# Sliding-window attention and a squared-ReLU feed-forward layer on one core: a planned schedule with other DMA figures, stores issued on ScalarE, and accumulator rows zeroed by VectorE

## The chip, the cores and the metric

The kernel runs on one core of a Trainium2 chip. The time is that of the device for one execution, in microseconds (us). A core has five engines with an instruction queue each: TensorE (PE in the profile, its weight loads PEld), VectorE (DVE), ScalarE (ACT), GpSimd (POOL) and SyncE (SP). Each works through its queue in order and waits on semaphores.

## The reference

```python
# q, k, v: 8 batches x 8 heads x 576 positions x 64, float32
scores = q @ k^T / 8                     # per batch and head
attn = softmax(scores where |i - j| <= 32, else -1e9)
a = attn @ v                             # 8 x 8 x 576 x 64
x = a.transpose(0, 2, 1, 3).reshape(4608, 512)
out = relu(x @ w_in)**2 @ w_out          # w_in 512 x 2048, w_out 2048 x 512; out 4608 x 512 float32
```

## The kernel before

**Groups.** The 4608 rows of x are cut into 24 groups of 192 queries (G = 0 to 23), three to a batch (b, g = divmod(G, 3)). Each group treats all eight heads. A group has two halves w of 128 keys: half A (w = 0) and half B (w = 1). Because of the window of 32 to either side, the 128 keys of a half meet at most 128 queries other than zero.

**Attention of a group.** `load_qk` and `load_v` (L319, L331) load two pieces each of K, Q and V from GpSimd, which casts them to bf16. Q and K have to be transposed. For the first two batches (G below 6) TensorE does it (`turn_pe`, L361); after that SyncE issues transposing DMAs (`turn_dma`, L389, two of K and two of Q per group). `scores` (L400) runs eight matmuls per half into one PSUM tile; ScalarE takes the exponential (L426) and VectorE multiplies by the mask (L431). `pv` (L434) multiplies by V, with a 65th column of ones that gives the sum of each row. Rows 64 to 127 of the result of half A are final for the first 64 queries; rows 0 to 63 go on to half B. VectorE takes reciprocals (L464) and normalises (L467) into `xa` and `xb`. Between the halves, rows 64 to 127 of the PSUM tile `avp` must be made empty, since half B accumulates onto it: two small matmuls with zeros and start=True, one for each bank, ahead of half B's eight (L444). `xturn` (L472) transposes the result into columns of `xt`: by TensorE for G below 6 (`NXT`), by two transposing DMAs on SyncE from there on (L496, L498).

**Feed-forward.** `mm1` (L503) is the first projection: chunks of 192 tokens up to 768, one of 256, then 512; four matmuls of 128 x 128 weights per 128 of the 2048 features. ScalarE does the ReLU (L521) out of two PSUM buffers `ht`, VectorE the square (L524) into `gt`. `mm2` (L528) is the second projection for 128 tokens (block u, 36 in all) in four segments of four matmuls, into two PSUM buffers `outp`; after the last segment ScalarE copies the result into `oe` (L545), one of three buffers, and SyncE issues its store (L547).

**The order.** Nothing is ordered by hand. `rec` records each operation with what it reads and writes, a key and an assumed duration. The keys count in units of 64 tokens: first projection at its token's unit, second at 2u + LAG (LAG = 9), scores and P V of G at 3G - LEAD (LEAD = 12), the loads of a group AHEAD = 6 units before its scores. `schedule` then plans a run: an engine that is free takes the ready operation of lowest key. From this plan each engine's instruction list is written out, with semaphore waits for the dependences; on the chip an engine follows its list, whatever is ready. In the plan a DMA lands 1700 ns after its last packet is moved, a transposing DMA occupies SyncE for 900 ns:

```python
                    it[3].end = now + 1700
                    done(it[3], it[3].end)
```

A load of the third batch or later also waits, by `after=self.moe`, for the scores or first-projection operation recorded last before it. In the trace the loads of a group start some 1.1 us after the scores of half A two groups before it. Matmuls on zeros (L265) keep TensorE busy in gaps near the start.

Of the kernel before, what the change touches and what calls it, by code (L numbers as in the profile page):

```python
# [20 lines left out]
NTURN = 2  # L21
NXT = 6
LEAD = 12.0
LAG = 9.0
AHEAD = 6.0
WARM = 40000
KC = ((0, 224), (224, 192), (416, 160))


class Op:  # L30
    __slots__ = ("eng", "fn", "deps", "order", "inc", "val", "sem", "dma", "dur", "key", "i",
                 "succ", "left", "ready", "start", "end", "lat", "move", "name")


class Prog:
# [8 lines left out]
        self.writer = {}  # L44
        self.readers = {}

    def rec(self, eng, fn, reads=(), writes=(), dma=None, dur=100, key=0.0, move=0, name="", after=None):
        op = Op()
        op.eng, op.fn, op.dma, op.dur, op.key, op.move, op.name = eng, fn, dma, dur, key, move, name
        op.deps, op.order = set(), set()  # L50
        op.inc, op.val, op.sem = False, None, None
        op.lat = self.LAT[eng]
        for r in reads:
            w = self.writer.get(r)
            if w is not None:
                op.deps.add(w)
        for t in writes:
            w = self.writer.get(t)
            if w is not None:
                (op.order if w.eng == eng and w.dma is None and dma is None else op.deps).add(w)  # L60
            for r in self.readers.get(t, ()):
                (op.order if r.eng == eng and r.dma is None else op.deps).add(r)
        if after is not None:
            op.deps.add(after)
        op.deps.discard(op)
        op.order.discard(op)
        for r in reads:
            self.readers.setdefault(r, []).append(op)
        for t in writes:
            self.writer[t] = op  # L70
            self.readers[t] = []
        op.i = len(self.ops)
        self.ops.append(op)
        return op

    def schedule(self):
# [27 lines left out]
        def serve(until):  # L104
            nonlocal now, spent
            while now < until:
                nxt = min((r[0][0] for r in rings.values() if r), default=None)
                if nxt is None or nxt >= until:
                    now = max(now, min(until, nxt) if nxt is not None and nxt < 1e12 else until)
                    return False  # L110
                now = max(now, nxt)
                for q in list(order):
                    if rings[q] and rings[q][0][0] <= now:
                        break
                it = rings[q][0]
                spent += it[2]
                if spent >= (180 if q == "POOL" else 60):
                    order.remove(q)
                    order.append(q)
                    spent = 0  # L120
                now += it[2]
                it[1] -= 1
                if it[1] <= 0:
                    rings[q].pop(0)
                    it[3].end = now + 1700
                    done(it[3], it[3].end)
                    return True
            return False
# [87 lines left out]
def act(n):  # L216
    return 175 + 0.833 * n
# [6 lines left out]
class Gen:  # L224
# [5 lines left out]
    def alloc(self):  # L230
        nc = self.nc
        sb, ps = nc.alloc_sbuf_tensor, nc.alloc_psum_tensor
        self.SC = ps("sc", [128, 1024], F32)
        self.AVP = ps("avp", [128, 1024], F32)
        self.HT = [ps(f"ht{i}", [128, 512], F32) for i in range(2)]
        self.OUTP = [ps(f"outp{i}", [128, 512], F32) for i in range(2)]

        self.RAW = {t: [sb(f"{t}raw{i}", [128, 2, 512], BF16) for i in range(NRAW)] for t in "qk"}
        self.QT = [sb(f"qt{i}", [128, 4, S_], BF16) for i in range(2)]
        self.KT = [sb(f"kt{i}", [128, 4, KW], BF16) for i in range(2)]  # L240
        self.V = [sb(f"v{i}", [128, 2, H_, VS], BF16) for i in range(NV)]
        self.DIF = sb("dif", [128, 128], F32)
        self.MASK = [sb(f"mask{i}", [128, 128], BF16) for i in range(4)]
        self.ID = sb("ident", [128, 128], BF16)
        self.E = [sb(f"e{i}", [128, 1024], BF16) for i in range(2)]
        self.PT = [sb(f"pt{i}", [128, 8, 128], BF16) for i in range(3)]
        self.RS = [sb(f"rs{i}", [128, 8], F32) for i in range(4)]
        self.XA = [sb(f"xa{i}", [128, 512], BF16) for i in range(3)]
        self.XB = [sb(f"xb{i}", [128, 512], BF16) for i in range(3)]
        self.XT = sb("xt", [128, 4, RING], BF16)  # L250
        self.W1 = sb("w1", [128, 4, DFF], BF16)
        self.W2 = sb("w2", [128, 16, DM], BF16)
        self.GT = sb("gt", [128, 16, RING], BF16)
        self.RT = [sb(f"rt{i}", [128, 512], BF16) for i in range(4)]
        self.ZZ = sb("zz", [128, 512], BF16)
        self.OE = [sb(f"oe{i}", [128, 512], F32) for i in range(3)]

    def ms(self, eng, t, ap, v, key, dur=120):
        return self.p.rec(eng, lambda e: e.memset(ap, v), writes=t, key=key, dur=dur)  # L259
# [59 lines left out]
    def load_qk(self, t, b, g, key):  # L319
        t0, n = KC[g] if t == "k" else (192 * g, 192)  # L320
        h = n // 2
        G = 3 * b + g
        raw = self.RAW[t][G % NRAW]
        src = (self.q if t == "q" else self.k)[b]
        s = src[:, t0:t0 + n, :].rearrange("h (j p) d -> p j h d", j=2)
        for j in range(2):
            self.p.rec("POOL", lambda e, j=j: e.dma_start(raw[0:h, j, :].rearrange("p (h d) -> p h d", h=8), s[:, j]),  # L327
                       writes=[("raw", t, G % NRAW, j)], dma=(f"{t}{G % NRAW}{j}", G), key=key, dur=500 + 3 * h,
                       move=(h // 2, 14.5), name=f"{t}{b}{g}{j}", after=self.moe if b > 1 else None)

    def load_v(self, b, g, key):  # L331
        G = 3 * b + g
        vt = self.V[G % NV]
        for j in range(2):
            k0 = 192 * g - 32 + 128 * j
            lo, hi = max(k0, 0), min(k0 + 128, S_)
            n = hi - lo
            self.p.rec("POOL", lambda e, j=j, lo=lo, hi=hi, k0=k0: e.dma_start(  # L338
                vt[lo - k0:hi - k0, j, :, 0:64], self.v[b, :, lo:hi, :].rearrange("h p d -> p h d")),
                writes=[("v", G % NV, j)], dma=(f"v{G % NV}{j}", G), key=key, dur=500 + 3 * n, move=(n // 2, 14.5),  # L340
                name=f"v{b}{g}{j}", after=self.moe if b > 1 else None)

    def load_w1(self, d, key):
        src = self.w_in[:, 512 * d:512 * d + 512].rearrange("(f p) c -> p f c", p=128)
# [44 lines left out]
    def turn_dma(self, t, b, g, key):  # L389
# [3 lines left out]
        for x in range(2):  # L393
            self.p.rec("SP", lambda e, x=x: e.dma_start(dst[:, :, h * x:h * x + h], raw[0:h, x, :], transpose=True),  # L394
                       reads=[("raw", t, G % NRAW, x)], writes=[(t + "t", b % 2, g) if x else (t + "h", b % 2, g)],
                       dma=(f"t{t}{G % 6}", G), key=key, dur=900, move=(h // 4, 20), name=f"td{t}{b}{g}")

# [34 lines left out]
    def pv(self, G, w):  # L434
# [4 lines left out]


        def f(e):
            if w:
                for x in range(2):
                    e.matmul(avp[64:128, 512 * x + 508:512 * x + 512], self.ZZ[:, 0:64], self.ZZ[:, 0:4], start=True, stop=True,  # L444
                             skip_group_check=True)
# [7 lines left out]
        if G % 3 != 1:  # L453
            rd.append(("vpad", G % NV))
        wr = ["av_hi"] if w else ["av_hi", "av_lo"]
        self.p.rec("PE", f, reads=rd + (["av_lo"] if w else []), writes=wr + (["av_lo"] if w else []), key=key,
                   dur=260 + 100 * w, name=f"P{G}{'AB'[w]}")
        lo = 64 * (1 - w)
        rs = self.RS[n % 4]
        x = (self.XB if w else self.XA)[G % 3]  # L460
# [7 lines left out]
                                                    av[:, :, :, 0:64], rb, ALU.mult),  # L468
                   reads=rd + [("rs", n % 4)], writes=[("xb" if w else "xa", G % 3)], key=key - 0.05,
                   dur=dve(512, False), name=f"N{G}{'AB'[w]}")  # L470

    def xturn(self, G):  # L472
        xa, xb = self.XA[G % 3], self.XB[G % 3]
# [3 lines left out]
        if G < NXT:  # L477
# [7 lines left out]
            def f1(e):  # L485
                for j in range(4):
# [7 lines left out]
                       reads=["av_hi", "av_lo"], writes=wr, key=key, dur=act(768), name=f"XT{G}")  # L494
            return
        self.p.rec("SP", lambda e: e.dma_start(self.XT[:, :, r:r + 64], xa[64:128, :], transpose=True),  # L496
                   reads=[("xa", G % 3)], writes=wr[:1], dma=(f"xa{G % 3}", G), key=key - 0.3, dur=900, move=(16, 20), name=f"T{G}a")
        self.p.rec("SP", lambda e: e.dma_start(self.XT[:, :, r + 64:r + 192], xb[:], transpose=True),  # L498
                   reads=[("xb", G % 3)], writes=wr[1:], dma=(f"xb{G % 3}", G), key=key, dur=900, move=(32, 20), name=f"T{G}b")

# [25 lines left out]
    def mm2(self, u, seg, key):  # L528
# [12 lines left out]
        if u == 1 and seg == 0:  # L541
            self.p.idle_end = o
        if seg == 3:
            oe = self.OE[u % 3]
            self.p.rec("ACT", lambda e: e.activation(oe[:], op[:], ACTF.Copy), reads=[f"outp{u % 2}"],  # L545
                       writes=[("oe", u % 3)], key=key, dur=act(512), name=f"o{u}")
            self.p.rec("SP", lambda e: e.dma_start(self.out[128 * u:128 * u + 128, :], oe[:]),  # L547
                       reads=[("oe", u % 3)], writes=[("out", u)], dma=(f"o{u % 3}", u), key=key, dur=600, move=(8, 80), name=f"st{u}")

    def build(self):  # L550
        p = self.p
# [102 lines left out]
```

## Time and profile before

| what | value |
|---|---|
| median of three runs (lowest, highest) | 331.99 us (328.82, 335.5) |
| the profiled execution, its time | 333.94 us |
| its span, first to last instruction | 331.6 us |
| mean granted TensorE clock | 0.984 |
| busy: PE, DVE, ACT, POOL | 315.9, 142.5, 163.6, 120.8 us |
| first projection L515, PE busy | 148.6 us, 768 matmuls |
| second projection L535, PE busy | 145.3 us, 576 matmuls |
| scores L416, P V L448, clears L444, PE busy | 19.3, 20.7, 5.4 us |

Busy time of PE adds modelled ends of pipelined matmuls, which overlap: four matmuls of 512 columns that stand as 1.03 us start 0.216 us apart and give way to the next after 0.86 us. The stage from 151.5 to 247.5 us is steady: a group takes 12 us. Before 57 us no transposing DMA is issued; the last two for Q are issued from 247.45 us on; from 314.8 us TensorE does the second projection alone.

### The profile page before, as it was taken

The page shows a single profiled execution, that of the slowest core. Times are in us where ns is not written, and L with a number is a line of the kernel's source. Part 1 is how long each engine was busy: PE and PEld are TensorE (multiplying, and loading weights), DVE is VectorE, ACT ScalarE, POOL GpSimd, SP SyncE. Part 2 cuts the span into 40 slices and gives each one's busy share as a digit, 9 for nine tenths or more (in the row PEclk, how much of TensorE's full clock was granted, in tenths as well). Part 3 has the DMA queues.
Part 4 walks back from the last instruction along what each step waited for, and adds up shares of the span by engine and source line. Part 5 has one row for each costly group of instructions (what it writes and reads, how often), then busy time and mean ns, then how long its engine had stood idle before and what let it go on. Part 6 is the DMA issues. An engine that isn't in the chain of part 4 may idle for free.

```text
span 331.6 us, 6027 instructions
## 1 busy us (share of the span) xinstructions
PE 315.9 (95%) x2359; PEld 161.7 (49%) x2359; DVE 142.5 (43%) x332; ACT 163.6 (49%) x249; POOL 120.8 (36%) x157
## 2 busy tenths in 40 slices
PE   8999999949997999889999999999999999999996
PEld 3457786725643444344444444444444444444442
DVE  6356355704644547435354355355445432222200
ACT  1357575813724657355446545635544644434312
POOL 8999305632745519055145225325400000000000
PEclk9999999969999799999999999999999999999999
DMA  9999998999999999999999999799993120010012
GB/s 71 178 171 206 184 172 85 107 170 112 83 157 155 173 146 152 144 141 153 163 148 119 126 143 139 116 140 135 124 155 96 37 57 32 32 65 32 32 65 95
DMA packets 175451, 39.86 MB, mean 120 GB/s; under 512 B 166720, under 2 KB 170816, under 8 KB 175424
## 3 DMA queue, kind: packets, MB, share of 16 engines
q0 software_dynamic: 125312, 19.41, 89.5%
q1 hardware_dynamic: 50112, 20.07, 33.2%
q8 instruction: 19, 0.31, 0.4%
q14 instruction: 8, 0.07, 0.1%
HBM read 38.80 MB, written 9.44 MB: 145 GB/s over the span
## 4 chain that ended last, share of the span: by engine, by line
PE 85%; DMA 7%; SPq 3%; DVE 2%; ACT 1%; issue 1%; POOL 0%; POOLq 0%
PE ht L515 37%; PE outp L535 34%; DMA qt<-qraw 6%; PE sc L416 5%; PE avp L448 4%; PE outp L265 3%; SPq L394 2%; DMA kraw<-in_k_dram 1%; PE avp L444 1%; DVE xa L467 1%; DVE pt L431 1%; PE sc L374 1%; SPq L498 1%; PE avp L487 0%; PE avp L482 0%
## 5 line engine op out<-in xcount | busy, mean ns | idle before, releaser
L515 PE MATMUL ht<-xt,w 128*128 128x512 bf16 (+2 forms) x768 | 148.6, 329 | 0.5 <-ACT rt L521 0.2
L535 PE MATMUL outp<-w,gt 128*128 128x512 bf16 x576 | 145.3, 382 | 0.0
L521 ACT ACTIVATE rt<-ht 128x512 bf16<-128x512 f32 (+1 forms) x152 | 87.5, 576 | 93.1 <-PE ht L515 89.7
L524 DVE TENSOR_TENSOR gt<-rt 128x512 bf16<-128x512 bf16 (+1 forms) x152 | 61.7, 409 | 91.7 <-ACT rt L521 91.2
L515 PEld LDWEIGHTS ht<-xt,w 128*128 128x128 bf16 x768 | 67.3, 98 | 49.1 <-issue 1.1
L535 PEld LDWEIGHTS outp<-w,gt 128*128 128x128 bf16 x576 | 54.2, 98 | 62.2 <-issue 1.7
L327 POOL DMA_DIRECT2D kraw<-in_k_dram x48 | 37.9, 808 | 119.8 <-PE sc L416 69.4
L426 ACT ACTIVATE e<-sc 128x1024 bf16<-128x1024 f32 x48 | 49.1, 1022 | 26.3 <-PE sc L416 26.3
L431 DVE TENSOR_TENSOR pt<-e,mask 128x1024 bf16<-128x1024 bf16 x48 | 33.1, 689 | 44.8 <-ACT e L426 44.4
L338 POOL DMA_DIRECT2D v<-in_v_dram x48 | 41.6, 891 | 0.0
L327 POOL DMA_DIRECT2D qraw<-in_q_dram x48 | 37.7, 807 | 0.0
L545 ACT ACTIVATE oe<-outp 128x512 f32<-128x512 f32 x36 | 21.5, 597 | 30.3 <-PE outp L535 27.2
L416 PE MATMUL sc<-qt,kt 64*128 64x128 bf16 x384 | 19.3, 220 | 10.4 <-DMA qt<-qraw 10.2
L416 PEld LDWEIGHTS sc<-qt,kt 64*128 64x128 bf16 x384 | 11.0, 95 | 29.1 <-issue 14.7
L464 DVE RECIPROCAL rs<-avp 64x8 f32<-64x8 f32 (+1 forms) x48 | 10.0, 209 | 26.9 <-PE avp L448 26.5
L448 PE MATMUL avp<-v,pt 128*128 128x65 bf16 x384 | 20.7, 196 | 0.0
L448 PEld LDWEIGHTS avp<-v,pt 128*128 128x128 bf16 x384 | 16.6, 99 | 5.7 <-DVE pt L431 0.6
L265 PE MATMUL outp<-zz 128*128 128x512 bf16 x55 | 16.9, 430 | 1.2 <-DVE zz L259 1.2
L467 DVE TENSOR_TENSOR xb<-avp,rs 128x512 bf16<-128x512 f32 x24 | 16.6, 690 | 1.2
L467 DVE TENSOR_TENSOR xa<-avp,rs 64x512 bf16<-64x512 f32 x24 | 16.7, 695 | 0.9
L265 PEld LDWEIGHTS outp<-zz 128*128 128x128 bf16 x55 | 5.2, 106 | 6.5 <-issue 2.5
L492 ACT ACTIVATE xt<-avp 128x768 bf16<-128x768 bf16 x6 | 4.9, 810 | 6.0 <-PE avp L487 5.9
(35 smaller groups left out, 49.9 us busy)
## 6 DMA issues: line engine op xcount, KB each, us to landing
out_dram<-oe SPq DMA_DIRECT2D x36, 256.0 KB, 2.6
qraw<-in_q_dram POOLq DMA_DIRECT2D x48, 96.0 KB, 5.5
v<-in_v_dram POOLq DMA_DIRECT2D x32, 128.0 KB, 6.8
w<-in_moe_w_in_dram POOLq DMA_DIRECT2D x4, 512.0 KB, 8.9
w<-in_moe_w_out_dram POOLq DMA_DIRECT2D x4, 512.0 KB, 15.4
kraw<-in_k_dram POOLq DMA_DIRECT2D x16, 112.0 KB, 4.7
v<-in_v_dram POOLq DMA_DIRECT2D x16, 96.0 KB, 6.0
kraw<-in_k_dram POOLq DMA_DIRECT2D x16, 96.0 KB, 5.3
```

The lines of the kernel that those rows point to most:

```text
L265: self.p.idle = lambda e: e.matmul(self.OUTP[1][:], self.ZZ[:, 0:128], self.ZZ[:], start=True, stop=True)
L327: self.p.rec("POOL", lambda e, j=j: e.dma_start(raw[0:h, j, :].rearrange("p (h d) -> p h d", h=8), s[:, j]), writes=[("raw", t, G % NRAW, ...
L338: self.p.rec("POOL", lambda e, j=j, lo=lo, hi=hi, k0=k0: e.dma_start(vt[lo - k0:hi - k0, j, :, 0:64], self.v[b, :, lo:hi, :].rearrange("h ...
L416: mm = e.matmul(sc[:, 512 * par + 128 * j:512 * par + 128 * j + 128], kt[r:r + 64, j, k0:k0 + 128], q, start=True, stop=True)
L426: self.p.rec("ACT", lambda e: e.activation(e_[:], sc[:], ACTF.Exp, scale=0.125), reads=["sc0", "sc1"], writes=[("e", n % 2)], key=key, dur ...
L431: self.p.rec("DVE", lambda e: e.tensor_tensor(pt[:], ee, mb, ALU.mult), reads=[("e", n % 2), ("mask", mi)], writes=[("pt", n % 3)], key=ke ...
L448: mm = e.matmul(avp[:, 512 * x + 65 * y:512 * x + 65 * y + 65], pt[:, 4 * (h % 2) + h // 2, :], vt[:, w, h, 0:65], start=(w == 0 and y == ...
L467: self.p.rec("DVE", lambda e: e.tensor_tensor(x[lo:128, :].rearrange("p (x y c) -> p x y c", x=2, y=4), av[:, :, :, 0:64], rb, ALU.mult), ...
L515: mm = e.matmul(ht[:, n * x:n * x + n], self.W1[:, ft, 128 * d:128 * d + 128], self.XT[:, ft, r:r + n], start=(ft == 0), stop=(ft == 3))
L521: self.p.rec("ACT", lambda e: e.activation(rt[:, 0:c], ht[:, 0:c], ACTF.Relu), reads=[f"ht{k % 2}"], writes=[("rt", k % 4)], key=key, dur= ...
L524: self.p.rec("DVE", lambda e: e.tensor_tensor(gt[:, d0:d0 + len(ds), r:r + n], rr, rr, ALU.mult), reads=[("rt", k % 4)], writes=[("gt", s, ...
L535: mm = e.matmul(op[:], gt[:, d, r:r + 128], self.W2[:, d, :], start=(d == 0), stop=(d == 15))
```

## The change

Five things are changed together.

1. The plan's figures for transposing DMAs: an issue takes 1290 ns (`TISS`) where it was 900, and a landing 2000 ns more (`TSLACK`). For loads of the third batch on, a landing takes 1500 ns more (`LSLACK`). These change the planned order alone; no instruction waits longer by them.
2. The two clearing matmuls stay for G below 6 (`NCLR`). From G = 6 a VectorE memset of rows 64 to 127 and 2 x 260 columns of `avp` stands in for them. It reads `xa`, so it follows half A's normalisation, and half B's P V waits for it.
3. The store of the output is issued by ScalarE instead of SyncE.
4. `oe` has four buffers instead of three.
5. LAG is 6 instead of 9.

```diff
-LAG = 9.0
+LAG = 6.0
 AHEAD = 6.0
+TISS = 1290
+TSLACK = 2000
+LSLACK = 1500
+NCLR = 6
...
-                    it[3].end = now + 1700
+                    it[3].end = now + 1700 + it[3].slack
...
-        self.OE = [sb(f"oe{i}", [128, 512], F32) for i in range(3)]
+        self.OE = [sb(f"oe{i}", [128, 512], F32) for i in range(4)]
...
-                       move=(h // 2, 14.5), name=f"{t}{b}{g}{j}", after=self.moe if b > 1 else None)
+                       move=(h // 2, 14.5), name=f"{t}{b}{g}{j}", after=self.moe if b > 1 else None, slack=LSLACK if b > 1 else 0)
...
-                       dma=(f"t{t}{G % 6}", G), key=key, dur=900, move=(h // 4, 20), name=f"td{t}{b}{g}")
+                       dma=(f"t{t}{G % 6}", G), key=key, dur=TISS, move=(h // 4, 20), name=f"td{t}{b}{g}", slack=TSLACK)
...
-            if w:
+            if w and G < NCLR:
                 for x in range(2):
                     e.matmul(avp[64:128, 512 * x + 508:512 * x + 512], self.ZZ[:, 0:64], self.ZZ[:, 0:4], start=True, stop=True,
                              skip_group_check=True)
...
-                   dur=260 + 100 * w, name=f"P{G}{'AB'[w]}")
+                   dur=260 + 160 * (w and G < NCLR), name=f"P{G}{'AB'[w]}")
...
+        if not w and G >= NCLR:
+            z = avp[64:128, :].rearrange("p (x c) -> p x c", x=2)[:, :, 0:260]
+            self.p.rec("DVE", lambda e: e.memset(z, 0.0), reads=[("xa", G % 3)], writes=["av_hi"], key=key - 0.05, dur=650, name=f"Z{G}")
...
-            oe = self.OE[u % 3]
+            oe = self.OE[u % 4]
...
-            self.p.rec("SP", lambda e: e.dma_start(self.out[128 * u:128 * u + 128, :], oe[:]),
-                       reads=[("oe", u % 3)], writes=[("out", u)], dma=(f"o{u % 3}", u), key=key, dur=600, move=(8, 80), name=f"st{u}")
+            self.p.rec("ACT", lambda e: e.dma_start(self.out[128 * u:128 * u + 128, :], oe[:]),
+                       reads=[("oe", u % 4)], writes=[("out", u)], dma=(f"o{u % 4}", u), key=key, dur=600, move=(8, 80), name=f"st{u}")
```

The two transposing DMAs of `xturn` get `TISS` and `TSLACK` in the same way.

More of the change, by code (lines that the diff above doesn't have):

```diff
@@ L31 @@
     __slots__ = ("eng", "fn", "deps", "order", "inc", "val", "sem", "dma", "dur", "key", "i",
-                 "succ", "left", "ready", "start", "end", "lat", "move", "name")
+                 "succ", "left", "ready", "start", "end", "lat", "move", "name", "slack")
 class Prog:
@@ L45, in __init__, with rec @@
         self.readers = {}
-    def rec(self, eng, fn, reads=(), writes=(), dma=None, dur=100, key=0.0, move=0, name="", after=None):
+    def rec(self, eng, fn, reads=(), writes=(), dma=None, dur=100, key=0.0, move=0, name="", after=None, slack=0):
         op = Op()
@@ L51, in rec @@
         op.inc, op.val, op.sem = False, None, None
+        op.slack = slack
         op.lat = self.LAT[eng]
@@ L340, in load_v @@
                 writes=[("v", G % NV, j)], dma=(f"v{G % NV}{j}", G), key=key, dur=500 + 3 * n, move=(n // 2, 14.5),
-                name=f"v{b}{g}{j}", after=self.moe if b > 1 else None)
+                name=f"v{b}{g}{j}", after=self.moe if b > 1 else None, slack=LSLACK if b > 1 else 0)
     def load_w1(self, d, key):
@@ L496, in xturn @@
         self.p.rec("SP", lambda e: e.dma_start(self.XT[:, :, r:r + 64], xa[64:128, :], transpose=True),
-                   reads=[("xa", G % 3)], writes=wr[:1], dma=(f"xa{G % 3}", G), key=key - 0.3, dur=900, move=(16, 20), name=f"T{G}a")
+                   reads=[("xa", G % 3)], writes=wr[:1], dma=(f"xa{G % 3}", G), key=key - 0.3, dur=TISS, move=(16, 20), name=f"T{G}a",
+                   slack=TSLACK)
         self.p.rec("SP", lambda e: e.dma_start(self.XT[:, :, r + 64:r + 192], xb[:], transpose=True),
-                   reads=[("xb", G % 3)], writes=wr[1:], dma=(f"xb{G % 3}", G), key=key, dur=900, move=(32, 20), name=f"T{G}b")
+                   reads=[("xb", G % 3)], writes=wr[1:], dma=(f"xb{G % 3}", G), key=key, dur=TISS, move=(32, 20), name=f"T{G}b", slack=TSLACK)
     def mm1(self, t0, n, ds, key):
@@ L543, in mm2 @@
         if seg == 3:
-            oe = self.OE[u % 3]
+            oe = self.OE[u % 4]
             self.p.rec("ACT", lambda e: e.activation(oe[:], op[:], ACTF.Copy), reads=[f"outp{u % 2}"],
-                       writes=[("oe", u % 3)], key=key, dur=act(512), name=f"o{u}")
-            self.p.rec("SP", lambda e: e.dma_start(self.out[128 * u:128 * u + 128, :], oe[:]),
-                       reads=[("oe", u % 3)], writes=[("out", u)], dma=(f"o{u % 3}", u), key=key, dur=600, move=(8, 80), name=f"st{u}")
+                       writes=[("oe", u % 4)], key=key, dur=act(512), name=f"o{u}")
+            self.p.rec("ACT", lambda e: e.dma_start(self.out[128 * u:128 * u + 128, :], oe[:]),
+                       reads=[("oe", u % 4)], writes=[("out", u)], dma=(f"o{u % 4}", u), key=key, dur=600, move=(8, 80), name=f"st{u}")
     def build(self):
```

## The prediction

> **What bounds the kernel now.** I read the page's busy row and clock row first, then the waits of TensorE, then the span cut into stages around those waits, then the order of time on TensorE, SyncE and GpSimd inside them.
>
> ```profile
> PE 315.9 (95%) x2359; PEld 161.7 (49%) x2359; DVE 142.5 (43%) x332; ACT 163.6 (49%) x249; POOL 120.8 (36%) x157
> PEclk9999999969999799999999999999999999999999
> PE sc L416 <- DMA qt<-qraw: 10.2, 3, 5.4
> 65.47:71.02 5.55, 0.17 (x2) 0.04 (x2) 0.89 (x3) 0.60 (x1) 0.83 (x1) 0.77 2.05 168
> 71.02:75.34 4.32, 4.32 (x30) 2.43 (x30) 1.50 (x4) 1.51 (x2) 3.31 (x5) 0.50 1.13 152
> 105.90:108.13 2.23, 0.06 (x1) 0.00 (x1) 1.27 (x3) 0.00 (x0) 0.85 (x2) 1.00 1.46 240
> 109.48:112.89 3.41, 3.41 (x18) 1.59 (x18) 2.54 (x6) 2.34 (x4) 3.41 (x5) 0.50 1.99 147
> 139.40:142.08 2.68, 0.00 (x1) 0.00 (x1) 0.43 (x1) 0.60 (x1) 0.00 (x0) 1.00 1.74 149
> ```
>
> TensorE is the bound: it is busy 95% of the span, and from 142 us to the last matmul it never waits. (A stage row gives from:to, length, busy us with counts for PE, PEld, DVE, ACT and POOL, then clock, DMA share and GB/s.) So a change is worth what it takes from TensorE's own list or from its holes. The holes after the start are three, all in front of a score group (L416) that waits for a transposed Q: 10.2 us together. After two of them the granted clock is 0.50 for 4.32 and 3.41 us.
>
> ```profile
> 52.35 0.40 PE L416 MATMUL sc<-qt,kt 64*128 64x128 bf16 x8
> 53.48 1.64 POOL L327 DMA_DIRECT2D kraw<-in_k_dram  x2 [17.38 <-PE sc L416]
> 57.21 6.16 SPq L394 DMA_TRANSPOSE kt<-kraw  x2
> 63.41 2.56 SPq L394 DMA_TRANSPOSE qt<-qraw  x2
> 64.61 1.03 PE L535 MATMUL outp<-w,gt 128*128 128x512 bf16 x4
> 71.02 0.61 PE L416 MATMUL sc<-qt,kt 64*128 64x128 bf16 x8 [5.38 <-DMA qt<-qraw]
> 108.13 0.40 PE L416 MATMUL sc<-qt,kt 64*128 64x128 bf16 x8 [2.18 <-DMA qt<-qraw]
> 142.08 0.40 PE L416 MATMUL sc<-qt,kt 64*128 64x128 bf16 x8 [2.68 <-DMA qt<-qraw]
> ```
>
> This is one chain from end to end. Group 4's scores at 52.35 release the loads of group 6 on GpSimd (53.48); SyncE issues two transposes of K, held by the loads, then two of Q, done at 65.97; Q lands about 5 us later and group 6's scores start at 71.02, 18.67 us after group 4's. TensorE had come to that place at 65.64, 13.3 us after 52.35. The instruction order is fixed before the run by a planner, so TensorE can't take other work in the hole although projection work was ready: at 65.5 it had done about 3.9 of the four 192-token chunks of the first projection and 3 token blocks (48 matmuls) of the second, of six whose inputs the first four chunks give.
>
> **The three stalls.** The planner's figures in the code are 900 ns for a transposing issue and 1700 ns from last packet to landing. The trace has 1254 ns:
>
> ```profile
> L394 SPq DMA_TRANSPOSE qt<-qraw x36: 1180/1254/2522, 63.4 to 247.4; - x36
> L547 SPq DMA_DIRECT2D out_dram<-oe x36: 332/519/1682, 42.8 to 329.3; - x36
> ```
>
> The diff plans 1290 ns an issue (4 in the chain, so 4 x 0.39 = 1.56 us), 1.5 us more for a load and 2.0 us more for a transpose: the planned chain grows by 5.06 us. It doesn't make data earlier; it moves the score group later in TensorE's list, behind work that is ready. Against 5.38, 2.18 and 2.68 us of lateness it leaves 0.32, 0 and 0. Bounds on the spread: transposes land after 2.3 us at best, 5.0 at the median, 8.5 at worst. The new plan allows 0.6 + 0.5 + 1.7 + 2.0 = 4.8 us, so the worst is 3.7 late, of which the load and issue margins (1.5 + 1.56) catch 3.06: 0.64 us an event. I take two such events, 1.3 us; the ends are 0 and all three stalls as before. So 10.24 - 0.32 - 1.3 = 8.6 us gained.
>
> **The clock behind them.** TensorE worked 4.32 and 3.41 us at 0.50: 2.16 + 1.70 = 3.86 us lost. Without the holes I take all of it back; the least is nothing. The Trainium skill, page "TensorE: Matmul & The Clock Gate", section "Part 1: The HAM clock gate", speaks against a part of this: it lets the clock halve only after at least one whole idle window of about 3.4 us. By that rule the 2.18 us hole did not cause the second half-clock stretch and 1.70 us of this term would stay; here the trace has the stretch 1.35 us after that hole, and I go by the trace.
>
> **Clearing matmuls.** Groups 6 to 23 lose their pair (L444). In the steady stage:
>
> ```profile
> 190.86 0.42 PE L448 MATMUL avp<-v,pt 128*128 128x65 bf16 x8
> 191.12 1.02 PE L535 MATMUL outp<-w,gt 128*128 128x512 bf16 x4
> 192.84 1.03 PE L535 MATMUL outp<-w,gt 128*128 128x512 bf16 x4
> 193.80 0.22 PE L444 MATMUL avp<-zz 128*64 128x4 bf16 x2
> 193.95 0.43 PE L448 MATMUL avp<-v,pt 128*128 128x65 bf16 x8
> 194.22 1.02 PE L515 MATMUL ht<-xt,w 128*128 128x512 bf16 x4
> ```
>
> Four 512-column matmuls start 0.216 us apart, so the group of 192.84 gives way at 193.70; P V starts at 193.95. The half without a clear follows its neighbour with no gap (190.86 to 191.12 is its own 0.26 us, as 193.95 to 194.22 is). A pair costs 0.25 us of TensorE: 18 x 0.25 = 4.5 us.
>
> Its stand-in is a VectorE memset of 64 partitions x 520 f32 in PSUM. No row shows one. The nearest are
>
> ```profile
> L467 DVE TENSOR_TENSOR xa<-avp,rs 64x512 bf16<-64x512 f32 x24 | 16.7, 695 | 0.9
> L259 DVE MEMSET v<- 32x264 uint32 x4 | 1.1, 278 | 0.2
> ```
>
> so 0.28 to 0.70 us; scaled from the memset, 278 x 520/264 = 0.55, which I take. 18 x 0.55 = 9.9 us on VectorE, 45 us busy in the 96 us from 151.5 to 247.5. It lies between the normalisation of half A and P V of half B: a new wait of one memset and a hand-over. In the steady stage A ends at 191.28 and B starts 193.95; reciprocal, normalisation and memset (0.21 + 0.70 + 0.55, with three hand-overs of about 0.1 to 0.2) end near 193.1. What it can hold on VectorE is the next half's mask multiply and a squaring; TensorE has three projection groups of 0.86 us there. I price it at nothing; with no cover 18 x 0.7 = 12.6 us. A gain is excluded.
>
> **Stores on ScalarE.** SyncE loses 36 issues of about 0.52 us (18.7 us) and the waits in front of them; ScalarE gets them, each behind its own copy (L545). SyncE then carries six transposes a group, 6 x 1.25 = 7.5 of 12 us, and the Q of the next groups no longer stands behind a store. Queued behind the store on ScalarE are the next ReLU (L521) and exponential (L426), for which TensorE waits through two buffers: 1.73 us per turn when both projections alternate, of which ScalarE uses 0.60. ScalarE is busy 51.0 of 96 us; 0.52 more in 8 us fits. I take nothing; with no cover 18.7 us, and the gain's end is 0, since the only wait for a store (3.2 us, ScalarE at 108.7) lay beside a stall of TensorE. The fourth output buffer only loosens that wait.
>
> **LAG 9 to 6** ranks the second projection three units (192 tokens) earlier. It moves work within a list that is full: the tail after the last first-projection group shrinks from 63 matmuls to about 51 (an estimate: three units are 24 matmuls, half of them met by first-projection work that goes later), and the same matmuls run before. Nothing; if the last squaring were late, the other output buffer holds 0.86 us groups to run. The start, up to the first transposing issue at 57.21, keeps its loads: the slack applies from the third batch on.
>
> **Sum.** -8.6 - 3.9 - 4.5 = -17.0 us. The profiled execution took 333.94 (span 331.6 and 2.3 around it), 1.95 above the median of 331.99. From the median: 315.0; from the profiled one: 316.9. I give **315.0**.
>
> **Rivals.** *The cover runs out* (0.12). From 92.87 to 101.3 TensorE has only the second projection to do, waiting for group 7's columns; then 12 of that work's matmuls are left, 2.6 us. If TensorE comes there 5.38 + 2.16 us sooner and the columns don't, a hole of about 5 us opens: 320. Against it: group 7's Q landed near 75.6 while its scores ran at 84.11, late only because the list had slid by those 7.5 us.
>
> *Holes or blocked evictions stay* (0.12). The margins miss, or half the store issues (9.4 us) land on TensorE's path: 322 to 327.5; the upper end is the clears alone, the change not doing what it says. For it: loads and transposes together took 8 us to land around 130.
>
> *The attention chain becomes the bound* (0.10), on the slower side. Each group's loads wait for the scores two groups before. That chain is 18.7 us at group 6 and up to 21 later; TensorE needs 24 us for two groups now and 23.5 after. If the planned chain exceeds 23.5, TensorE starves once the ready work is used: at 26 us it loses 2.5 us in each of 8.5 links from group 6 to 23, 21 us, and -17 + 21 makes 336. Its point is 23.5 us, and 18.7 to 21 real plus margins that mostly equal the real lateness keep under it.
>
> The **forecast** has 0.66. Its own range is 310 (all 18.6 us and the lowest run's 328.8) to 319. To hold 8 in 10 I go up to 326, which takes in the cover case and most of the third. 2% is 6.6 us, about what a measurement of this kernel can tell from no change: faster 0.79, same 0.12, slower 0.09.
>
> **What would show it.** Right: no wait of L416 on Q over 1 us, clock 1.00 from 30 us on, 12 clearing matmuls, a group period near 11.75 us from 150 us on. Wrong: waits of P V on a memset, of L515 on ReLUs behind store issues, of L515 on transposed attention columns near 95 us, or a group period above 12 us.

## The result, and the profile after

The changed kernel takes 317.31 us (median of four runs, 316.5 to 318.14) where the kernel before takes 332.56 (328.82 to 335.5) on the same chip: a ratio of 0.958, interval 0.949 to 0.967. In a later comparison it was 317.08 against 329.77, ratio 0.964 (0.959 to 0.969). Here and below a ratio leaves out runs more than 1.5% above the fastest of their kernel, so it is not quite the quotient of the medians. The change takes 13 to 15 us; the forecast was 17, and 315.0 lies 2.3 us below the measured median. The profiled execution took 316.6 us with a span of 314.4.

The page's busy row and clock row, then the waits of TensorE on other engines, the longest first. Lines have moved by a few: scores are L421, clears L449, P V L453, the first projection L524, the second L544.

```profile
PE 303.9 (97%) x2284; PEld 158.8 (51%) x2322; DVE 149.7 (48%) x350; ACT 162.8 (52%) x249; POOL 120.6 (38%) x157
PEclk9999999999999999999999999999999999999999
PE outp L379 <- DMA kraw<-in_k_dram: 1.6, 2, 1.0
PE outp L270 <- DVE zz L264: 1.2, 1, 1.2
PE ht L524 <- issue: 0.8, 5, 0.2
```

No wait of scores on Q is left, and the clock is full in every slice. The waits on loads and on the zeros are those of the start. The rows that end with "issue" are gaps of 0.2 us: this trace has 2284 matmuls to 2322 weight loads, so 38 matmul records are missing, and such a gap is about one matmul long. In order of time, the place where the kernel before stood still for 5.38 us (groups 5 and 6):

```profile
67.96 0.43 PE L453 MATMUL avp<-v,pt 128*128 128x65 bf16 x8
68.22 1.89 PE L544 MATMUL outp<-w,gt 128*128 128x512 bf16 x8
...
71.36 1.03 PE L544 MATMUL outp<-w,gt 128*128 128x512 bf16 x4
72.32 0.40 PE L421 MATMUL sc<-qt,kt 64*128 64x128 bf16 x8
```

Group 6's scores start at 72.32, later than the 71.02 of before. The list now has P V of group 5 and second-projection work in front, and TensorE works through what was a hole.

The memset and its neighbours in the group and wait rows, and in order of time:

```profile
L478 DVE MEMSET avp<- 64x520 f32 x18 | 8.9, 492 | 2.3 <-DVE xa L472 0.9
PEld avp L453 <- DVE avp L478: 1.6, 6, 0.3
166.50 1.03 PE L524 MATMUL ht<-xt,w 128*128 128x512 bf16 x4
167.36 0.42 PE L453 MATMUL avp<-v,pt 128*128 128x65 bf16 x8
167.83 0.81 PE L544 MATMUL outp<-w,gt 128*128 128x512 bf16 x3
```

It takes 0.49 us (0.55 estimated). P V follows the projection with no gap in front (166.50 to 167.36 is four matmuls), as forecast. From 167.36 to 167.83 it seems to take 0.47 us instead of 0.26, but the group behind it has three matmuls where there are always four: the first one's record is missing. The second profile of the changed kernel has as many matmuls as weight loads (2322), and the same place in it reads

```profile
166.53 1.03 PE L524 MATMUL ht<-xt,w 128*128 128x512 bf16 x4
167.39 0.42 PE L453 MATMUL avp<-v,pt 128*128 128x65 bf16 x8
167.65 1.02 PE L544 MATMUL outp<-w,gt 128*128 128x512 bf16 x4
```

with 0.26 us, as before. In six of 18 groups the weight load of P V waited for the memset, 1.6 us together, but P V itself started late by 0.1 us at most.

Two-group spacing of scores shows who sets the pace. In the stage from 150 us on the kernel before kept 12.0 us a group, the pace of TensorE's list. Now group 14's scores are at 152.00 and group 16's at 172.89, 20.9 us for two: attention runs ahead of TensorE's need, and group 23's scores come at 247.64 instead of 259.49. Only the last two steps, from group 21 to 23, are even, 11.74 and 11.75 us.

### The profile page after: what moved, and what is told of

Read it like the earlier page. It is cut to its first block, busy times and chain, and to the rows that moved or that the text cites. A ratio compares the mean times of both kernels' runs of the same rounds, so it can differ in the third digit from the quotient of the medians.

```text
span 314.4 us, 5936 instructions
## 1 busy us (share of the span) xinstructions
PE 303.9 (97%) x2284; PEld 158.8 (51%) x2322; DVE 149.7 (48%) x350; ACT 162.8 (52%) x249; POOL 120.6 (38%) x157
## 4 chain that ended last, share of the span: by engine, by line
PE 86%; DMA 6%; POOL 3%; issue 1%; DVE 1%; ACT 1%; SPq 1%; ACTq 0%; POOLq 0%
PE ht L524 38%; PE outp L544 37%; PE sc L421 5%; PE avp L453 4%; DMA qt<-qraw 3%; DMA qraw<-in_q_dram 3%; POOL kraw L332 1%; SPq L399 1%; POOL qraw L332 1%; PE sc L379 1%; PE outp L270 1%; POOL v L343 1%; POOL w L350 0%; PE avp L495 0%; ACT rt L530 0%
## 5 line engine op out<-in xcount | busy, mean ns | idle before, releaser
L524 PE MATMUL ht<-xt,w 128*128 128x512 bf16 (+2 forms) x754 | 143.9, 325 | 1.3 <-issue 0.8
L544 PE MATMUL outp<-w,gt 128*128 128x512 bf16 x555 | 138.7, 379 | 1.3 <-issue 0.3
L533 DVE TENSOR_TENSOR gt<-rt 128x512 bf16<-128x512 bf16 (+1 forms) x152 | 60.8, 406 | 72.3 <-ACT rt L530 71.4
L524 PEld LDWEIGHTS ht<-xt,w 128*128 128x128 bf16 x768 | 67.3, 98 | 50.6 <-ACT rt L530 1.3
L544 PEld LDWEIGHTS outp<-w,gt 128*128 128x128 bf16 x576 | 53.4, 98 | 59.8 <-ACT oe L554 1.3
L453 PEld LDWEIGHTS avp<-v,pt 128*128 128x128 bf16 x384 | 17.5, 98 | 9.8 <-DVE avp L478 1.6
L453 PE MATMUL avp<-v,pt 128*128 128x65 bf16 x384 | 20.1, 194 | 0.3 <-DVE pt L436 0.3
L421 PE MATMUL sc<-qt,kt 64*128 64x128 bf16 x384 | 19.1, 219 | 0.4 <-ACT qt L388 0.3
L421 PEld LDWEIGHTS sc<-qt,kt 64*128 64x128 bf16 x384 | 10.9, 94 | 16.9 <-issue 8.2
L270 PE MATMUL outp<-zz 128*128 128x512 bf16 x51 | 15.1, 420 | 1.4 <-DVE zz L264 1.2
L478 DVE MEMSET avp<- 64x520 f32 x18 | 8.9, 492 | 2.3 <-DVE xa L472 0.9
```

Source lines behind the costliest of these rows:

```text
L421: mm = e.matmul(sc[:, 512 * par + 128 * j:512 * par + 128 * j + 128], kt[r:r + 64, j, k0:k0 + 128], q, start=True, stop=True)
L453: mm = e.matmul(avp[:, 512 * x + 65 * y:512 * x + 65 * y + 65], pt[:, 4 * (h % 2) + h // 2, :], vt[:, w, h, 0:65], start=(w == 0 and y == ...
L524: mm = e.matmul(ht[:, n * x:n * x + n], self.W1[:, ft, 128 * d:128 * d + 128], self.XT[:, ft, r:r + n], start=(ft == 0), stop=(ft == 3))
L533: self.p.rec("DVE", lambda e: e.tensor_tensor(gt[:, d0:d0 + len(ds), r:r + n], rr, rr, ALU.mult), reads=[("rt", k % 4)], writes=[("gt", s, ...
L544: mm = e.matmul(op[:], gt[:, d, r:r + 128], self.W2[:, d, :], start=(d == 0), stop=(d == 15))
```

## The experiments

The theory: TensorE's own work plus the holes in its list is the time; a hole is the lateness of transposed Q, K or attention columns against the planned order; the clock halves after some holes. Rivals: SyncE's queue is what is late; the memset gives back elsewhere what the clears cost; the long chain of attention is the bound.

### Single parts on the kernel before

The plan's figures alone:

```diff
+TISS = 1290      # dur of the four transposing DMA records, 900 before
+TSLACK = 2000    # their slack
+LSLACK = 1500    # slack of loads from the third batch on
-                    it[3].end = now + 1700
+                    it[3].end = now + 1700 + it[3].slack
```

> The kernel before with the plan's figures alone (1290 ns issues, 2000 and 1500 ns slack); clears, stores on SyncE, three output buffers and LAG 9 as before. The prediction's own sum: the three holes before scores and the half clock after them go, -12.5 us, near 320 us where the kernel before has 332; no wait of scores on Q over 1 us. Rival (SyncE's queue is what is late, because stores and their waits stand among the transposes): holes of several us stay, 326 to 332.

Measured 320.38 us against 329.83 for the kernel before, ratio 0.974 (0.970 to 0.979). Its profile has no wait of scores on a DMA at all. The holes and the clock behind them are cured by order alone, with every store still on SyncE; the rival falls as the main cause. The gain is 9.5 us and not 12.5. The three figures were changed together; which of them is needed is not shown.

The memset alone, for the clears of groups 6 to 23:

```diff
-            if w:
+            if w and G < NCLR:
...
+        if not w and G >= NCLR:
+            z = avp[64:128, :].rearrange("p (x c) -> p x c", x=2)[:, :, 0:260]
+            self.p.rec("DVE", lambda e: e.memset(z, 0.0), ...
...
-                   dur=260 + 100 * w, name=f"P{G}{'AB'[w]}")
+                   dur=260 + 160 * (w and G < NCLR), name=f"P{G}{'AB'[w]}")
```

The last lines are the planned duration of P V, which goes with the clears; it changes the order alone.

> The kernel before with VectorE's memset in place of the clears from group 6 on, and nothing else. The prediction's sum: 18 x 0.25 = 4.5 us less TensorE work, 327.5 where the kernel before has 332, if the three holes keep their 10.2 us. Rival (a change of the order moves the holes as well): a time outside 325 to 330, with holes whose sum differs from 10.2 us by as much.

Measured 330.12 us, ratio 1.000 (0.996 to 1.004): nothing. The sum's 327.5 fails; the time lies at the upper edge of the rival's range, and the holes did move. The work did leave TensorE: half A's scores of groups 16 and 17 in its steady stage are

```profile
173.21 0.40 PE L421 MATMUL sc<-qt,kt 64*128 64x128 bf16 x8
184.95 0.40 PE L421 MATMUL sc<-qt,kt 64*128 64x128 bf16 x8
```

11.74 us apart, the 0.26 us less that the clears' price says. It came back in holes and clock (waits, one row of the order of time, and one stage row, whose last three figures are clock, DMA share and GB/s):

```profile
PE sc L421 <- DMA qt<-qraw: 6.2, 3, 3.8
PE ht L524 <- DMA xt<-xb: 2.5, 2, 2.1
127.21 3.57 PE L524 MATMUL ht<-xt,w 128*128 128x512 bf16 x8 [2.10 <-DMA xt<-xb]
127.28:130.70 3.42, 3.42 (x11) 1.23 (x12) 0.00 (x0) 0.60 (x1) 3.38 (x5) 0.50 2.41 154
```

A new hole before the first projection waits for transposed attention columns, and half clock follows it; another 6.8 us of half clock stand at the hole of 3.8 us before scores. Over the runs of this comparison the mean granted clock is 0.983 with the memset (the 11 runs of its ratio) and 0.994 without (18 runs); one minus the clock, times the span, is 5.5 against 1.9 us. So up to 3.6 of the 4.5 us went to the clock (these figures count idle time at half clock too, which costs nothing). The rest may be longer holes, but a single profile can't show that.

Stores on ScalarE, four output buffers and LAG 6 together, plan's figures and clears as before:

```diff
-LAG = 9.0
+LAG = 6.0
-            oe = self.OE[u % 3]
+            oe = self.OE[u % 4]
-            self.p.rec("SP", lambda e: e.dma_start(self.out[...
+            self.p.rec("ACT", lambda e: e.dma_start(self.out[...
```

> The kernel before with stores on ScalarE, four output buffers and LAG 6; plan's figures and clears as before. The prediction's sum: nothing, 330 to 334, the holes before scores still there (10 us). Rival (SyncE freed of stores is the cure): holes under 5 us together, 320 to 326.

Measured 326.88 us, ratio 0.993 (0.989 to 0.997). Between the two expectations: 3 us gained, where I priced nothing. Its profile, of the fastest of twelve executions, has 2.0 us of waits of scores on Q, and 0.9 us on columns.

### The changed kernel less one part

The old plan's figures:

```diff
-TISS = 1290
-TSLACK = 2000
-LSLACK = 1500
+TISS = 900
+TSLACK = 0
+LSLACK = 0
```

> The changed kernel with the old plan's figures (900 ns, no slack). The prediction's sum: it loses the 12.5 us of holes and clock again, near 329.5. Rival (freed SyncE and moved stores have already made Q punctual): 317 to 322.

Measured 325.31 us against 329.83 for the kernel before (ratio 0.985, 0.979 to 0.991), some 8 us above the changed kernel of the next comparison (where the kernel before has 329.77). That lies between the two expectations: the old figures bring back 8 us, not 12.5. Its profile, of one of its two longest executions (327.21 us), has 4.7 us of waits of scores on Q. The other three were run beside the changed kernel on one chip, itself unedited:

> The changed kernel once more, as the measure for the three beside it: 314 to 318 where the kernel before has 330 to 332.

Measured 317.08 us.

```diff
-NCLR = 6
+NCLR = 24                                  # clears in all groups, no memset
...
-                   dur=260 + 160 * (w and G < NCLR), name=f"P{G}{'AB'[w]}")
+                   dur=260 + 100 * w, name=f"P{G}{'AB'[w]}")
```

> The changed kernel with the clearing matmuls back in all groups and no memset. By the prediction's term 18 x 0.25 us: 4.5 us slower than the changed kernel, group period 0.25 us longer. Rival (the memset gives back on another wait what the clears cost, as the kernel before with the memset alone suggests, which gained nothing): within 1.5 us of the changed kernel.

Measured 322.56 us (ratio to the kernel before 0.980, 0.973 to 0.986), 5.5 above the changed kernel. Executions of both at a mean clock of 0.999 or more have spans of 318.8 to 320.8 and 314.1 to 315.2, with medians 4.5 us apart. The group period came as expected too, where it is even: half A's scores of groups 22 and 23 stand 11.75 us apart in the changed kernel's first profile, and those of groups 21 and 22 12.00 here:

```profile
235.89 0.40 PE L421 MATMUL sc<-qt,kt 64*128 64x128 bf16 x8
247.64 0.40 PE L421 MATMUL sc<-qt,kt 64*128 64x128 bf16 x8
230.55 0.40 PE L421 MATMUL sc<-qt,kt 64*128 64x128 bf16 x8
242.55 0.40 PE L421 MATMUL sc<-qt,kt 64*128 64x128 bf16 x8
```

The price of 4.5 us holds, once no hole takes it back; the rival, drawn from the memset alone, holds for the old order only.

```diff
-            self.p.rec("ACT", lambda e: e.dma_start(self.out[...
+            self.p.rec("SP", lambda e: e.dma_start(self.out[...
```

> The changed kernel with its stores issued on SyncE again, all else as changed. By the prediction's price of nothing: within 1 us of the changed kernel. Rival (freeing SyncE is part of the cure, since stores on ScalarE, four buffers and LAG 6 alone took 3 us from the kernel before): 2 to 4 us slower, with waits of scores on Q.

Measured 319.85 us (ratio 0.972, 0.966 to 0.978), 2.8 above the changed kernel, with these rows in its profile:

```profile
119.28 0.40 PE L421 MATMUL sc<-qt,kt 64*128 64x128 bf16 x8 [0.73 <-DMA qt<-qraw]
131.74 0.40 PE L421 MATMUL sc<-qt,kt 64*128 64x128 bf16 x8 [0.66 <-DMA qt<-qraw]
```

Scores wait for Q again with the stores between the transposes. The price of nothing was wrong. The profile is of the fastest execution, 1.05 us above the fastest of the changed kernel, and its two waits make 1.4 us. The other executions have no profile; by their mean clocks they lost at most 1.2 us to the clock on average, against 0.1 in the changed kernel. The fourth output buffer was not tried by itself.

```diff
-LAG = 6.0
+LAG = 9.0
```

> The changed kernel with LAG 9. By the prediction's price of nothing: within 1 us of the changed kernel. Rival (the second projection ranked earlier leaves first-projection work as cover where group 7's columns come late): 2 to 4 us slower, with a wait of the first projection near 95 us.

Measured 319.40 us (ratio 0.972, 0.966 to 0.977), 2.3 above. The wait is of the expected kind, but at 129.78 us and not near 95:

```profile
129.78 1.90 PE L524 MATMUL ht<-xt,w 128*128 128x512 bf16 x8 [1.27 <-DMA xt<-xb]
```

With the larger LAG the first projection stands earlier in the list and meets columns that haven't landed. That this one wait and its like are the whole 2.3 us is not shown.

### The kernel before once more, and its loads earlier

Without an edit:

> The kernel before once more, for a second profile of its holes: 10 us of waits of scores on Q as in the first profile if that execution was typical; fewer, and fewer half-clock stretches, if it was a bad one, since its 333.94 us lay above the 329.8 us median of the later runs.

Measured 329.44 us. The profiled execution has a span of 326.6, and these waits (one row each of waits and of the order of time, then the stage behind):

```profile
PE sc L416 <- DMA qt<-qraw: 5.6, 4, 2.6
97.49 0.40 PE L416 MATMUL sc<-qt,kt 64*128 64x128 bf16 x8 [1.92 <-DMA qt<-qraw]
97.81:101.23 3.42, 3.42 (x12) 1.04 (x8) 1.12 (x2) 1.62 (x2) 2.65 (x4) 0.50 1.05 158
137.20 0.40 PE L416 MATMUL sc<-qt,kt 64*128 64x128 bf16 x8 [2.63 <-DMA qt<-qraw]
```

5.6 us of holes and one half-clock stretch (1.7 us lost), where the first profile had 10.2 and two (3.86). The first profile was of a bad execution. The other two waits of the second are 0.57 and 0.45 us long.

```diff
-AHEAD = 6.0
+AHEAD = 9.0
```

> The kernel before with its loads keyed 9 instead of 6 units before their scores, and nothing else: three groups instead of two in the chain, so the data come earlier while the plan's figures stay wrong. If lateness against the list is the cause, the holes close without any better figures: 318 to 322. Rival (SyncE's order itself, too many transposes planned at 900 ns, is the limit): holes of several us stay, 325 to 332.

Measured 322.96 us, ratio 0.979 (0.973 to 0.985), and its waits begin so:

```profile
PE outp L374 <- DMA kraw<-in_k_dram: 1.8, 3, 1.4
PE outp L265 <- DVE zz L259: 1.2, 1, 1.2
PE outp L535 <- issue: 1.1, 7, 0.2
```

No wait of scores on Q, in the fastest of four executions (320.16 us). The median lies 1 us above the range expected and 2 us below the rival's. Lateness against the list has two sides: data sooner cures it as well as a later place. The rival falls a second time as the main cause. This version of the changed kernel was not tried.

### Beyond the change

```diff
-TSLACK = 2000
+TSLACK = 9000
```

> The changed kernel with 9000 instead of 2000 ns of slack for a transposing DMA: the planned two-group chain, 20 to 21 us in the changed kernel's trace, becomes 27 to 28, beyond the 23.5 us that TensorE needs for two groups. By the prediction's third rival: TensorE starves by about 4 us for each two groups once the ready work is used, 8.5 links less a reserve of some two groups: 330 to 350, with waits on planned idle, not on late data. If the point of 23.5 us is wrong and the lead covers it: 316 to 322.

Measured 338.34 us, ratio 1.029 (1.022 to 1.036) to the kernel before. Half A's scores of groups 14 and 16 stand 27.1 us apart, as expected (first two rows; then the stage with the most idle time, and the longest hole):

```profile
172.50 0.40 PE L421 MATMUL sc<-qt,kt 64*128 64x128 bf16 x8
199.59 0.40 PE L421 MATMUL sc<-qt,kt 64*128 64x128 bf16 x8
110.00:143.00 33.00, 24.75 (x178) 12.09 (x180) 14.26 (x30) 12.53 (x18) 12.09 (x16) 0.93 1.32 131
142.97 3.19 PE L524 MATMUL ht<-xt,w 128*128 128x512 bf16 x7 [4.10 <-DMA xt<-xb]
```

So the slower side existed, and 338 lies near the 336 of the prediction's third rival. That is chance: its sum charges each of 8.5 links what the chain exceeds 23.5 us by. For 27.1 us that is 3.6 x 8.5 = 30.6 us, or 348 from the changed kernel's 317. The loss is not spread over the links. Between 110 and 143 us alone TensorE is idle for 8.25 us, in the stretch where ready work runs out before the next 512 columns arrive; between the scores at 172.50 and 199.59 it is hardly idle (26.78 busy of 27.10). Part of the holes, 5.4 us before scores and 5.0 us before the first projection in its waits, are real waits on late data again, against my expectation of planned idle alone. P V waits for the memset here, 3.0 us in two places. And the clock, 0.975 over a span of 334.8 us, took at most 8.4 us.

```diff
-NCLR = 6
+NCLR = 0
```

> The changed kernel with the memset in all 24 groups (no clearing matmuls). If a pair costs 0.25 us of TensorE everywhere: 6 x 0.25 = 1.5 us less, 315.5. Rival (in the first 60 us TensorE waits for loads and fills with matmuls on zeros, so nothing is on its path, and the memset lengthens the chain from load to first projection): no change or up to 1 us slower.

Measured 320.21 us, ratio to the kernel before 0.973 (0.968 to 0.978), where the changed kernel has 0.964: some 3 us slower, which neither expectation had. Its profile shows a hole in the list, for which the trace names nothing that ended it, and half clock behind it (order of time, then the stage):

```profile
131.66 2.31 PE L524 MATMUL ht<-xt,w 128*128 128x512 bf16 x8 [2.04 <-issue]
132.99:136.40 3.41, 3.41 (x16) 1.18 (x15) 1.54 (x3) 1.93 (x4) 1.47 (x3) 0.50 1.30 286
```

P V waits for the memset here too, 0.8 us in three places. Group 6's scores start at 74.00 us, 1.7 us later than in the changed kernel, but its first loads also came later (2.6 against 1.6 us of waits for K). Which part of the 3 us comes from the first 60 us and which from the hole isn't settled: its executions at a clock of 0.999 or more have spans of 316.8 to 317.6, some 2 us above those of the changed kernel. No version here beats the changed kernel.

## Why the prediction was right, and where it wasn't

**The bound and the main mechanism** held: TensorE's list with its holes is the time; the plan's figures move score groups behind ready work; holes and half clock go. The plan alone shows it, and the earlier loads show that it is lateness in the main; the stores in SyncE's queue are a smaller part of it (below). Of the signs named for it three came: no wait of scores on Q over 1 us, the clock at 1.00, and 12 clearing matmuls.

**The size of holes and clock** is the term that was too large. I put 8.6 + 3.86 = 12.5 us on it from one execution, which at 333.94 us was among the longest of its kernel, and subtracted that from a median. In the second profile it is 5.6 + 1.7 = 7.3 us, and the plan alone gained 9.5. Taken from the span of the second profile, 7.3 us for this term and 4.5 for the clears are 11.8 of the 12.2 us between 326.6 and the 314.4 of the changed kernel. So this term can account for the difference between my 17 us and the 13 of the later comparison.

**The clears** were right at 0.25 us a pair: 11.74 us a group in the steady stage with the memset alone, 4.5 us in the spans at full clock. What the prediction did not say is that the term depends on the first: while holes stay, less work only brings TensorE to them sooner. By itself the memset gained nothing, and up to 3.6 us went to the clock.

**The memset at nothing** was right for this order: 0.49 us, hidden but for 0.1 us. With other orders P V did wait for it, 0.3 us with LAG 9 and 3.0 us with the long chain.

**Stores and LAG at nothing** was the step with a wrong mechanism. I argued that ScalarE had room (it had) and that freeing SyncE bought nothing because the one wait for a store lay beside a stall. I named that Q no longer stands behind a store, but gave it no price: about 0.52 us per store in a queue of six 1.25 us transposes per group. Together these parts gained 3 us by themselves; taken out of the changed kernel, stores cost 2.8 and LAG 2.3. Why LAG does is only argued.

**The parts don't add.** Put in singly they give 9.5 - 0.3 + 3.0 = 12.2 us against 12.7 together, which looks like a sum; but taken out singly (with the clears at 5.5) they cost 8 + 5.5 + 2.8 + 2.3 = 18.6. In part they work on the same holes: stores, buffers and LAG alone left 2.9 us of them, at full clock. And that 315.0 came within 2.3 us is in part luck: my gain was 4.3 us too large against the later comparison, while the median of three that I took it from, 331.99, was 2.2 us above that comparison's 329.77.

**The cover** held: the first matmuls that need group 7's columns stand at 94.92 us, without a wait, with second-projection work in front of them. The columns came sooner as well: the last transposing issue for them ends at 89.62 us, before at 95.16. **The tail** has 52 matmuls (one of them without a record) where I put about 51, but by chance. Before, it had 76, from 311.98 us on, and not 63 or a start at 314.8; three units of LAG took all 24 matmuls out of it and not half. **The sign I named for the right outcome, a group period near 11.75 us from 150 us on**, was wrong: attention runs ahead in pairs at its own pace of some 21 us. The period shows in the last groups, and with the memset alone from group 14 on.

**The slower rival** was a sound one: a longer planned chain does make the kernel slower, by 21 us with 27.1 us. That the point lies at 23.5 us is not shown, and the sum behind its price does not hold.

## What to carry to other kernels

Where instruction lists are fixed before the run, a planner's wrong latency costs a hole on the bound engine though ready work stands behind it; plan with the durations and landings that the trace shows, but not with much more: 2 us of slack on transposes, with the two smaller corrections, closed the holes, and 9 us made the kernel slower than before. Changes that work on the same holes don't add, so take each out of the finished kernel as well as putting it in. Close the holes first: work taken off the bound engine turned into waits and half clock while they were there, and into time afterwards. Size a term of stalls from several executions, or say that it is one execution's.

## What the runs showed of the hardware that was not expected

Half clock follows holes well below 3.4 us, and not by their length: after holes of 1.92, 2.04, 2.10 and 2.18 us the granted clock was 0.50 for 3.41 us, after 2.63 and 2.68 us it was not. Such a stretch costs 1.7 us of TensorE's work, nearly as much as the hole itself. What came before tells them apart better. These are the 3.42 us in front of the stretches behind the holes of 1.92 and 2.10 us (the first number after the length is TensorE's busy time):

```profile
94.39:97.81 3.42, 1.50 (x14) 0.58 (x12) 0.00 (x0) 0.00 (x0) 0.00 (x0) 1.00 1.68 162
123.86:127.28 3.42, 1.32 (x15) 0.49 (x12) 3.00 (x6) 1.57 (x3) 3.42 (x5) 1.00 1.22 135
```

In front of the other two it was busy 1.35 us (hole of 2.18) and 1.37 us (2.04). In the first profile the clock changed at 68.52, 75.34, 109.48 and 112.89 us, whole multiples of 3.41 us apart. Cut by the same steps, the holes of 2.63 and 2.68 us are split over two stretches, and the less busy one still has 1.57 and 1.53 us. That is no threshold: with the clears back, half clock at 18.25 us follows a stretch with 1.61 us.

The Trainium skill, "TensorE: Matmul & The Clock Gate", section "Part 1: The HAM clock gate", asks for an idle window of about 3.4 us; the measurement decides against that as a lower limit.

A memset of 64 x 520 f32 into PSUM took 492 ns. A weight load of P V that waited for the memset did not delay the matmuls where it still ran in front of them: 0.26 us for P V with and without that wait.
